# Softmax per 4 MB chunk read from PSUM, longer rows, fewer slots and a re-ordered head and tail in a one-core decode-attention kernel

## The chip, the cores and the metric

The kernel runs on one core of one Trainium2 chip. The metric is the device time of the whole program in microseconds, the median of several runs. The profile gives a span from the first to the last instruction, which is about 1.8 us shorter than the time (672.71 against 670.9 us for the kernel before).

Names used below. PE is the engine for matrix products, DVE the vector engine, ACT the scalar engine, SP the engine that issues the loads. "K31" and "V31" are the last 4 MB chunks of the two caches. A "landing" is the moment at which a load's completion count is full. A "tile" is 128 keys by 128 values. "P.V" is the product of the softmax weights P with V. The "early heads" are query heads 0 to 27, the "late heads" 28 to 31.

## The reference, cut to what matters

One token attends to a cache of 65,536 keys with 8 cache heads and 4 query heads for each. K and V together are 268 MB in bf16, and each byte is used once. The weights add 12 MB.

```
xn = layernorm(x)                                   # 512 values
q  = xn @ wq                                        # 32 heads of 128
scores = einsum(q, K) / sqrt(128);  p = softmax(scores)
o  = einsum(p, V)
out = x + o @ wo + (gelu(xn @ w1 + b1) @ w2 + b2)   # 512 values
```

## The kernel before

A small recording layer gives every operation its semaphore waits; the PE program of the steady state is folded into a hardware loop. For each tile of K, PE transposes it into PSUM, DVE or ACT copies it to SBUF, and PE multiplies it with the four queries. P.V uses each V tile as the weights. All loads are issued by SP, in order, as slots come free.

Before, K and V come in chunks of 2 MB (16 KB per partition), four of each make a unit, and softmax statistics are formed per unit of 256 tiles:

```python
BPC = 2; TPD = BPC * TPB; NC = 4                     # 64 tiles per chunk, 4 chunks per unit
slot = [kv[:, i*TPD*DH:(i+1)*TPD*DH] ... for i in range(2 * NC)]      # 8 slots of 2 MB

def scores(u, blk):
    ... pe.matmul(pss[sb][:, col*HPG:(col+1)*HPG], lhsT=kt_ring[...], rhs=q_cur) ...
    if blk % BPS == BPS - 1:
        dve.tensor_copy(out=scf[k][:, ...], in_=pss[sb])              # PSUM -> SBUF
        dve.tensor_reduce(out=pmax_parts[...], in_=dst, op=max)
...
# after the last unit (tail), in PE's order:
stats_1(); stats_2(L)
pv(0, 0); pv(0, 1)                                   # P.V of the last unit, chunk by chunk
... weights of all heads on DVE ...
pv(1, 0); pv(1, 1)
pv(2, 0)
wo_part(oT_bf, "oT", list(range(H)))                 # 128 matmuls
pv(2, 1); pv(3, 0); pv(3, 1)
... oL, wo_part of the last four heads, transpose, copy, store ...
```

## Time and profile before

| | before |
|---|---|
| time, median of 3 runs | 672.94 us (672.90 to 673.02) |
| span of the profiled run | 670.9 us |
| bytes read from HBM | 280.5 MB |
| PE busy | 83% |
| first load packet / last landing | 2.0 us / 665.2 us |
| tail after the last landing | 5.7 us |

The first lines are from the profile page of the kernel before: the busy time of each engine, and the rate of the loads in 40 equal slices of the span.

```profile
span 670.9 us, 27090 instructions
...
PE 556.9 (83%) x12746; PEld 540.2 (81%) x12746; DVE 288.2 (43%) x512; ACT 243.9 (36%) x325; POOL 1.3 (0%) x10
...
GB/s 375 414 424 422 427 422 425 429 427 429 420 420 429 425 429 413 426 431 427 426 415 425 430 425 428 415 426 430 427 426 430 428 427 426 428 427 428 427 429 206
```

The rate is flat: the loads are the bound, and only the first and the last slice are short. The stretches view says the same with finer windows. (In windows of a few microseconds it counts a packet whole, so that shares of 1.04 and 440 GB/s can appear, as from 5 to 10 us.) Its columns are the window in us, its length, the busy us and number of instructions of each engine, then the granted clock of PE, the busy share of the load engines, and GB/s.

```profile
core 0: us, PE busy (x) PEld busy (x) DVE busy (x) ACT busy (x) POOL busy (x), PEclk, DMA share, GB/s
100.00:200.00 100.00, 95.09 (x2091) 92.28 (x2089) 49.80 (x86) 43.54 (x59) 0.00 (x0) 0.77 1.01 425
...
500.00:600.00 100.00, 85.62 (x1953) 83.37 (x1952) 44.62 (x76) 40.33 (x56) 0.00 (x0) 0.78 1.01 427
...
655.00:660.00 5.00, 3.27 (x106) 3.18 (x103) 1.57 (x8) 0.00 (x0) 0.00 (x0) 0.50 1.00 423
660.00:665.00 5.00, 4.66 (x174) 4.67 (x175) 0.16 (x1) 0.00 (x0) 0.00 (x0) 0.50 0.47 193
```

The share is about 1 until 660 us. PE was not saturated: the waits view has it waiting for K chunks (columns: who waited for whom, us in total, times, longest).

```profile
PE pst L484 <- DMA kv<-in_A_k_cache_dram: 54.6, 22, 4.8
```

The last lines come from the timeline of PE and its neighbours at the end of the kernel before (columns: start, length, engine, line, operation; in brackets the idle time just before and what ended it).

```profile
660.34 1.02 PE L573 MATMUL pO<-P_bf,kv 128*128 128x4 bf16 x32 [2.07 <-DMA kv<-in_A_v_cache_dram]
...
664.63 2.70 PE L573 MATMUL pO<-P_bf,kv 128*128 128x4 bf16 x96
...
667.36 0.16 DVE L784 TENSOR_TENSOR oL_bf<-pO,coef 128x4 bf16<-128x4 f32 x1 [2.40 <-PE pO L573]
...
669.35 0.35 SPq L794 DMA_DIRECT2D out_dram<-fin_bf  x1
```

The wait for a V chunk ends at 660.34. The last 64 of the 96 matmuls at 664.63 are those of the chunk that landed at 665.2; they end at 667.3. The rest, to 670.9, is the last projection, the copy and the store.

The records of single load packets in the trace give the cost of a packet. This table is worked out from them; it is not a view of the profile.

```
kernel before: packet size, count, duration in ns
     4 B (completion count)    2164   median 9
  1024 B (wo)                  4096   min 46, median 48
 14336 B (w1, w2)               256   min 535, median 539
 16384 B (K, V)               16384   611 before compute starts; median 614, mean 616.7 over all
 32768 B (wq)                   128   1213 each
```

These fit 9 ns plus 27.2 GB/s for each of 16 load engines: an estimate from the table, since 2 x 611 - 1213 = 9 and 16,384 B in the other 602 ns are 27.2 GB/s.

### The profile page before, as it was taken

What the parts mean: (1) busy time and instruction counts of PE and PEld (TensorE: products, weight loads), DVE (VectorE), ACT (ScalarE), POOL (GpSimd) and SP (SyncE); (2) the same over time, 40 slices, a digit from 0 to 9 for tenths busy, and PEclk for the clock granted to TensorE, in tenths of its full rate; (3) what the DMA queues carried; (4) which work ended last, traced back from release to release, by engine and by line L of the source; (5) the groups of instructions that cost most, each with busy time, mean ns of one, the idle gap of its engine ahead of it and who ended that gap; (6) DMA issues with size and microseconds to landing.
All of it is one profiled execution on the core that took longest, in us unless ns stands there. A gap on an engine that the chain in (4) does not pass through costs nothing.

```text
span 670.9 us, 27090 instructions
## 1 busy us (share of the span) xinstructions
PE 556.9 (83%) x12746; PEld 540.2 (81%) x12746; DVE 288.2 (43%) x512; ACT 243.9 (36%) x325; POOL 1.3 (0%) x10
## 2 busy tenths in 40 slices
PE   0899979999998979779797788978889897898777
PEld 0898878989897878779787788877879787798766
DVE  0445434545554435345353444434444353454431
ACT  0233515353532425234261523515334161533330
POOL 0000000000000000000000000000000000000000
PEclk9876767979776778767687886678867797767965
DMA  8999999999999999999999999999999999999994
GB/s 375 414 424 422 427 422 425 429 427 429 420 420 429 425 429 413 426 431 427 426 415 425 430 425 428 415 426 430 427 426 430 428 427 426 428 427 428 427 429 206
DMA packets 23347, 280.82 MB, mean 419 GB/s; under 512 B 2458, under 2 KB 6556, under 8 KB 6556
## 3 DMA queue, kind: packets, MB, share of 16 engines
q1 hardware_dynamic: 23032, 280.50, 98.9%
q8 instruction: 15, 0.25, 0.1%
q10 hardware_dynamic: 292, 0.01, 0.0%
q14 instruction: 8, 0.07, 0.0%
HBM read 280.50 MB, written 0.00 MB: 418 GB/s over the span
## 4 chain that ended last, share of the span: by engine, by line
DMA 54%; PE 39%; ACT 6%; issue 1%; ACTq 0%; DVE 0%; SPq 0%
DMA kv<-in_A_k_cache_dram 49%; PE pst L484 26%; PE pO L573 5%; PE pss L505 5%; ACT P_bf L557 4%; DMA rows_bf<-in_B_b_dram 2%; ACT kt_ring L494 2%; DMA kv<-in_A_v_cache_dram 2%; PE pA L538 1%; PE pA L770 1%; PE pA L606 1%; PE pA L591 0%; PE pA L633 0%; ACTq L445 0%; PE pA L788 0%
## 5 line engine op out<-in xcount | busy, mean ns | idle before, releaser
L484 PE MATMUL pst<-ident_bf,kv 128*128 128x128 bf16 x4096 | 332.9, 255 | 80.1 <-DMA kv<-in_A_k_cache_dram 54.6
L484 PEld LDWEIGHTS pst<-ident_bf,kv 128*128 128x128 bf16 x4096 | 306.7, 117 | 90.6 <-issue 32.4
L494 ACT ACTIVATE kt_ring<-pst 128x1024 bf16<-128x1024 bf16 x192 | 194.7, 1022 | 381.7 <-PE pst L484 381.7
L492 DVE COPY kt_ring<-pst 128x1024 bf16<-128x1024 bf16 x320 | 213.1, 688 | 266.0 <-PE pst L484 265.6
L573 PE MATMUL pO<-P_bf,kv 128*128 128x4 bf16 x4096 | 117.1, 165 | 10.4 <-DMA kv<-in_A_v_cache_dram 4.9
L505 PE MATMUL pss<-q_cur,kt_ring 128*128 128x4 bf16 x4096 | 122.9, 165 | 1.4 <-issue 1.4
L573 PEld LDWEIGHTS pO<-P_bf,kv 128*128 128x128 bf16 x4096 | 111.8, 99 | 10.9 <-DMA kv<-in_A_v_cache_dram 5.2
L505 PEld LDWEIGHTS pss<-q_cur,kt_ring 128*128 128x128 bf16 x4096 | 118.7, 98 | 1.5 <-issue 1.5
L557 ACT ACTIVATE P_bf<-scf,negm 128x256 bf16<-128x256 f32 x64 | 49.6, 862 | 7.2 <-DVE negm L551 7.2
L513 DVE COPY scf<-pss 128x512 f32<-128x512 f32 x32 | 22.1, 692 | 64.5 <-PE pss L505 64.5
L517 DVE TENSOR_REDUCE pmax_parts<-scf 128x4 f32<-128x512 f32 x32 | 34.2, 1070 | 1.1
L457 PE MATMUL pA<-st,ones_f 128*128 128x2 f32 x2 | 0.6, 349 | 18.6 <-DVE st L455 18.6
L457 PEld LDWEIGHTS pA<-st,ones_f 128*128 128x128 f32 x2 | 0.5, 310 | 18.6 <-issue 18.6
L557 ACT ACTIVATION_READ_ACCUMULATOR P_bf<-scf,negm 128x1 f32 x64 | 13.6, 213 | 0.0
L538 PE MATMUL pA<-ident_f,pmax 128*4 128x128 f32 x32 | 8.5, 364 | 0.4 <-DVE pmax L525 0.4
L450 DVE CAST xT_f<-xT_bf 128x4 f32<-128x4 bf16 x1 | 0.2, 170 | 17.9 <-DMA rows_bf<-in_B_b_dram 17.9
L548 PEld LDWEIGHTS pA<-diag,ones_f 4*128 4x128 f32 x32 | 4.9, 190 | 2.7 <-DVE diag L542 1.1
L548 PE MATMUL pA<-diag,ones_f 4*128 4x4 f32 x32 | 6.3, 264 | 0.6 <-DVE diag L542 0.6
L468 ACT ACTIVATE mom<-mom 128x1 f32<-128x1 f32 x1 | 0.2, 203 | 16.3 <-DVE mom L466 16.3
L540 DVE TENSOR_REDUCE gmax<-pA 4x1 f32<-4x128 f32 x16 | 4.3, 269 | 0.6 <-PE pA L538 0.6
L582 DVE COPY o_all<-pO 128x4 f32<-128x4 f32 x15 | 2.3, 153 | 4.5 <-PE pO L573 4.5
L538 PEld LDWEIGHTS pA<-ident_f,pmax 128*4 128x4 f32 x32 | 1.4, 84 | 3.2 <-DVE kt_ring L492 2.5
(63 smaller groups left out, 50.1 us busy)
## 6 DMA issues: line engine op xcount, KB each, us to landing
kv<-in_A_k_cache_dram SPq DMA_DIRECT2D x64, 2048.0 KB, 31.6
kv<-in_A_v_cache_dram SPq DMA_DIRECT2D x64, 2048.0 KB, 33.8
kv<-in_A_wq_dram SPq DMA_DIRECT2D x1, 4096.0 KB, 17.1
wo_sb<-in_A_wo_dram SPq DMA_DIRECT2D x4, 1024.0 KB, 36.7
kv<-in_B_w_dram SPq DMA_DIRECT2D x2, 1792.0 KB, 27.7
xT_bf<-in_A_x_dram ACTq DMA_DIRECT2D x1, 1.0 KB
b1T_bf<-in_B_b_dram ACTq DMA_DIRECT2D x1, 3.5 KB
rows_bf<-in_A_x_dram ACTq DMA_DIRECT2D x1, 1.0 KB
```

What stands on the lines that cost most here:

```text
L484: lambda tb=tb, at=at, b=b, tt=s * TPB + t: pe.transpose(pst[tb][:, at * 128:(at + 1) * 128], slot[b][:, tt, :], ident_bf[:, :]),
L492: e, fn = DVE, lambda tb=tb, dst=dst: dve.tensor_copy(out=dst, in_=pst[tb][:, :])
L494: e, fn = ACT, lambda tb=tb, dst=dst: act.activation(out=dst, in_=pst[tb][:, :], func=ACTF.Copy)
L505: lambda sb=sb, col=col, kb=kb, t=t: pe.matmul(pss[sb][:, col * HPG:(col + 1) * HPG], lhsT=kt_ring[:, kb * BCOL + t * 128:kb * BCOL + (t + ...
L513: sch.op(DVE, lambda sb=sb, dst=dst: dve.tensor_copy(out=dst, in_=pss[sb][:, :]), reads=[f"pss{sb}"], writes=[f"scf{k}_{sb}"])
L517: lambda sb=sb, dst=dst: dve.tensor_reduce(out=pmax_parts[:, sb * HPG:(sb + 1) * HPG], in_=dst.rearrange("p (t j) -> p j t", j=HPG), axis= ...
L538: sch.op(PE, lambda: pe.matmul(pA[0:HPG, PA_ST:PA_ST + 128], lhsT=pmax[:, 0:HPG], rhs=ident_f[:, :], start=True, stop=True), reads=["pmax" ...
L548: sch.op(PE, lambda: pe.matmul(pA[:, PA_SB:PA_SB + HPG], lhsT=ones_f[0:HPG, 0:128], rhs=diag4[0:HPG, 0:HPG], start=True, stop=True), reads ...
L557: lambda k=k, u=u, j=j: act.activation(out=P_v[:, :, j], in_=scf_v[k][:, :, j], func=ACTF.Exp, bias=negm[:, u * HPG + j:u * HPG + j + 1], ...
L573: lambda b=b, tt=tt, gt=gt: pe.matmul(pO[:, 0:HPG], lhsT=slot[b][:, tt, :], rhs=P_v[:, gt, :], start=gt == 0, stop=gt == TPU - 1),
L606: lambda fc=fc, kt=kt: pe.matmul(pA[:, PA_H + fc:PA_H + fc + 1], lhsT=w1_sb[:, kt, fc:F:FC], rhs=xnT_bf[:, kt:kt + 1], start=kt == 0, stop ...
L770: lambda kt=kt, k=k, h=h: pe.matmul(pA[:, PA_AT + kt:PA_AT + kt + 1], lhsT=wo_sb[:, h, kt * 128:(kt + 1) * 128], rhs=rhs[:, k:k + 1], star ...
```

## The change

Its intent: fewer and longer load packets; no copy of the scores (the maximum and the exponentials read PSUM directly); PE starts on the first K chunk without waiting for layer norm; the last two V chunks use whatever slots are free; and the very last chunk arrives in pieces of 64, 32, 16, 8 and 8 tiles, so that little work is left after the last byte. The diff, cut to its core:

```diff
-    BPC = 2
+    BPC = 4                      # 128 tiles = 4 MB per chunk, 32 KB rows
-    NSLOT = 2 * NC               # 8 slots of 2 MB
+    NSLOT = 4                    # 4 slots of 4 MB
+    LASTP = (64, 32, 16, 8, 8)
+            if (kind, u) == ("V", NU - 1):      # last V chunk in falling pieces
+                for i, n in enumerate(LASTP):
+                    sch.dma(SP, ... slot[b][:, t0:t0 + n, :] ..., lsem[i], ...)
...
-            dve.tensor_copy(out=dst, in_=pss[sb][:, :])
-            dve.tensor_reduce(out=pmax_parts[...], in_=dst ...)
+            dve.tensor_reduce(out=pmax[:, :], in_=pss[k][:, 0:CW] ...)
-                    out=P_v[:, :, j], in_=scf_v[k][:, :, j], func=ACTF.Exp, ...   # 64 of 256 columns
+                    out=P_v[k][:, :, j], in_=src[:, :, j], func=ACTF.Exp, ...     # 128 of 128, from PSUM
...
+    # pair(i): two K chunks, two V chunks; the first pair transposes K before layernorm()
...
+    weights_1(*early)            # tail: "early" = heads 0 to 27, "late" = heads 28 to 31
+    stats_1()
+    weights_2(*early)
+    stats_2(L)
+    weights_3(*early)
+    merged(*early)
+    wo_part(*early)              # 112 matmuls
+    weights_1(*late)
+    pv(L - 1, range(TPD))        # P.V of V30
+    keep_o(L - 1)
+    ...
+    for i in range(len(LASTP)):  # P.V of V31, piece by piece
+        pv(L, range(cuts[i], cuts[i + 1]), f"last{i}")
+        if i == 0: wo_part(*late)
+        ...
```

## The prediction

> **What bounds the kernel now.** The DMA stream. In the stretches view the DMA share is 1.00 to 1.02 from 5 us to 660 us at 423 to 428 GB/s; 280.5 MB at that rate are 656 us of a 671 us span. The page's slices agree: only the first (375 GB/s) and last (206) are short. PE is 83% busy, but in the waits view it waited 54.6 us for K chunks, so it has slack. The queue never ran dry: a chunk's issue to landing was 7.8 us at least, 32 at the median. [...] So time per packet, the start and the tail count.
>
> **Time per packet.** In the trace's DMA packet records a 16 KB row took 611 ns before compute began and 616.7 ns on average later; the 32 KB rows of wq took 1213 ns each (all 128). 2 x 611 - 1213 = 9 ns, the time of one packet as such; a 4-byte semaphore packet also took 9 ns, and 1 KB took 46. So time = 9 ns + bytes at 27.2 GB/s per engine fits all sizes.
>
> **What the change does.**
> 1. 4 MB chunks with 32 KB rows: 16384 packets become 8192 on 16 engines: 8192 x 9 ns / 16 = 4.6 us less, and 64 fewer semaphore packets per engine, 0.6 us. If the 5.7 ns that compute adds to a packet is per packet rather than per byte, 2.9 us more. The last chunk's small pieces give 0.3 us back. Estimate: -6 us (-4.5 to -8).
> 2. Tail. The last piece landed at 665.2 us; 64 P.V matmuls ended at 667.3, the span at 670.9: 5.7 us. After: 8 P.V matmuls (estimate 0.4 us), oL 0.25, 16 matmuls of 128 columns at the half clock granted from 645 us on (1 to 1.9), one copy 0.35, out DMA 1.6. Estimate 4.4 us: -1.3 us.
> 3. Softmax from PSUM: 22 us of copies leave DVE, and exp becomes 128 x 256-to-128 column pieces, which adds some 20 us to ACT. Off the chain: 0.
> 4. K transposes first: PE starts at about 12 instead of 18.6 us. DMA is already queued for 38 us (16.2 MB), so 0 gained and nothing lost.
> 5. Four 4 MB slots: K(u+2) must be issued within about 29 us of K(u)'s landing; transposes take 8 (full clock) to 14 us (half clock). Some 13 us of slack remain: 0.
> 6. Start: first packet stays near 2.0 us: 0 to -0.5.
>
> **Predicted:** 672.9 - 6 - 1.3 = 665.6 us, range 662.5 to 669. Faster by over 2% (below 659.5) 6%, within 2% 92%, slower by over 2% 2%.
>
> **What would show it right.** 32 KB packets at 1216 to 1226 ns; steady rate 429 to 431 GB/s in the middle stretches; last landing near 659 to 660 us; 4 to 4.8 us after it; PE still waits for K chunks.
>
> **What would make it wrong.** If 32 KB rows under compute took 1233 ns (2 x 616.7), only the tail would be left: 671. If they ran at 1213 throughout, and the tail fell to 3 us, 659. If coarse slots let the queue run dry (DMA share below 0.97 in a middle stretch), slower. The 16 engines finish the last chunk between 661.2 and 665.2 us: if this skew shrinks or grows, the end moves by up to 2 us.

Remarks on it. "1.00 to 1.02 at 423 to 428 GB/s" holds for the stretches between 20 and 650 us; the short windows near the start show 0.98 to 1.04 and 420 to 440. With the bytes of each packet record spread over its duration, these windows give 428 to 432 GB/s. Last, its two clocks: in the trace of the kernel before, the clock records read 0.50 from 645.0 us to the end, and a transpose started every 55.9 ns at a granted clock of 1.00 and every 106.6 ns at 0.50, which is 7.2 and 13.6 us for the 128 of a chunk.

## The result and the profile after

| | before | after |
|---|---|---|
| time, median | 672.97 us (4 runs) | 671.02 us (670.45 to 671.21, 4 runs) |
| ratio | | 0.997 (0.9952 to 0.9987) |
| span of the profiled run | 670.9 us | 669.4 us |
| last landing | 665.2 us | 660.0 us |
| tail after it | 5.7 us | 9.4 us |

A ratio is the mean time of one kernel's fast runs over that of the other's in the same rounds, so it is not quite the ratio of the medians. The kernel is 0.3% faster; 665.6 us had been forecast.

The same lines of the page and of the stretches view, for the changed kernel:

```profile
span 669.4 us, 27324 instructions
...
PE 555.8 (83%) x12818; PEld 525.2 (78%) x12818; DVE 264.1 (39%) x548; ACT 243.5 (36%) x455; POOL 1.3 (0%) x10
...
GB/s 376 420 436 423 434 425 430 431 431 433 417 429 435 429 433 414 433 429 435 431 415 435 429 431 431 417 429 433 429 433 435 427 433 433 431 429 435 426 423 106
```

```profile
100.00:200.00 100.00, 91.49 (x2016) 86.20 (x2014) 43.79 (x86) 40.06 (x73) 0.00 (x0) 0.77 1.01 429
...
500.00:600.00 100.00, 86.41 (x1971) 81.69 (x1971) 41.08 (x82) 38.89 (x76) 0.00 (x0) 0.76 1.00 431
...
655.00:660.00 5.00, 2.95 (x111) 2.89 (x109) 0.63 (x6) 0.21 (x1) 0.00 (x0) 0.50 0.45 173
660.00:665.00 5.00, 4.95 (x162) 4.56 (x159) 1.77 (x13) 0.00 (x0) 0.00 (x0) 0.50 0.02 7
```

The five stretches from 100 to 600 us moved 425 to 427 GB/s before and 428 to 431 after, against a forecast of 429 to 431. The loads end early: in the stretch 660 to 665 the share is 0.02, where it was 0.47. In that same stretch PE is busy for 4.95 of 5 us. The packet records say why the stream is shorter: 32 KB packets took 1216 ns at the median and 1220.7 on average, and the durations of all K and V packets, the small pieces included, sum to 625.4 us per engine, against 631.5 before. The last landing came 5.2 us sooner. (The records overlap a little, as the share just above 1 shows, so their sum is not the time of the stream.)

PE still waits for K chunks, 88.8 us in all, of which 13.1 are for the very first chunk:

```profile
PE pst L477 <- DMA kv<-in_A_k_cache_dram: 88.8, 25, 13.1
```

The gain was lost behind the last landing. The granted clock of PE was 0.50 in both tails, so it does not make the difference. The timeline of PE in the tail of the changed kernel, with the two vector operations it turns on:

```profile
647.13 0.59 PE L518 MATMUL pA<-ident_f,pmax 128*4 128x128 f32 x2
...
648.41 0.77 PE L729 MATMUL pA<-sums,ones_f 128*128 128x112 f32 x2 [0.70 <-DVE gmax L520]
...
649.11 0.58 PE L528 MATMUL pA<-diag,ones_f 4*128 4x4 f32 x2
...
652.06 0.18 DVE L754 CAST oT_bf<-o_sum 128x28 bf16<-128x28 f32 x1
...
652.30 3.15 PE L763 MATMUL pA<-oT_bf,wo_sb 128*128 128x1 bf16 x112 [2.60 <-DVE oT_bf L754]
...
655.31 2.27 PE L552 MATMUL pO<-P_bf,kv 128*128 128x4 bf16 x80
...
659.63 1.42 PE L552 MATMUL pO<-P_bf,kv 128*128 128x4 bf16 x48 [2.05 <-issue]
...
660.91 0.59 PE L729 MATMUL pA<-sums,ones_f 128*128 128x16 f32 x2
...
661.34 1.85 PE L552 MATMUL pO<-P_bf,kv 128*128 128x4 bf16 x64
...
663.69 0.99 PE L552 MATMUL pO<-P_bf,kv 128*128 128x4 bf16 x32
...
665.15 1.01 PE L552 MATMUL pO<-P_bf,kv 128*128 128x4 bf16 x32
666.20 0.16 DVE L799 TENSOR_TENSOR oL_bf<-pO,coef 128x4 bf16<-128x4 f32 x1 [2.17 <-PE pO L552]
...
666.41 0.60 PE L803 MATMUL pss<-wo_sb,oL_bf 128*1 128x128 bf16 x16 [0.25 <-DVE oL_bf L799]
...
667.38 0.61 SPq L813 DMA_DIRECT2D out_dram<-fin_bf  x1
```

V30 landed at 650.03 us. PE did not touch it until 655.31: it stood idle from 649.70 to 652.30, because the next operation in its order was the output projection of the 28 early heads (L763, 112 matmuls), and that waited for DVE's merged vector, finished at 652.24. Then came its 3.15 us. After 80 of V30's 128 matmuls PE stood again for 2.05 us with the cause "issue". When the last piece landed at 660.02, PE still had part of V30 and all of V31 before it. It reached the end of V31 at 666.16, 6.1 us late.

### The profile page after: what moved, and what is told of

Read it like the earlier page. It is cut to its first block, busy times and chain, and to the rows that moved or that the text cites. A ratio compares the mean times of both kernels' runs of the same rounds, so it can differ in the third digit from the quotient of the medians.

```text
span 669.4 us, 27324 instructions
## 1 busy us (share of the span) xinstructions
PE 555.8 (83%) x12818; PEld 525.2 (78%) x12818; DVE 264.1 (39%) x548; ACT 243.5 (36%) x455; POOL 1.3 (0%) x10
## 4 chain that ended last, share of the span: by engine, by line
DMA 56%; PE 39%; issue 2%; ACT 1%; DVE 1%
DMA kv<-in_A_k_cache_dram 56%; PE pst L477 27%; PE pss L497 5%; PE pO L552 3%; PE pA L518 1%; PE pA L528 1%; PE pA L763 1%; PE pA L570 1%; PE pA L585 1%; ACT kt_ring L487 0%; PE pA L612 0%; ACT P_bf L538 0%; ACT L538 0%; ACT L462 0%; PE pA L729 0%
## 5 line engine op out<-in xcount | busy, mean ns | idle before, releaser
L477 PE MATMUL pst<-ident_bf,kv 128*128 128x128 bf16 x4096 | 314.5, 246 | 90.4 <-DMA kv<-in_A_k_cache_dram 88.8
L477 PEld LDWEIGHTS pst<-ident_bf,kv 128*128 128x128 bf16 x4096 | 286.3, 112 | 109.7 <-DMA kv<-in_A_k_cache_dram 77.7
L552 PE MATMUL pO<-P_bf,kv 128*128 128x4 bf16 x4096 | 120.4, 165 | 11.7 <-issue 11.7
L552 PEld LDWEIGHTS pO<-P_bf,kv 128*128 128x128 bf16 x4096 | 113.8, 100 | 12.6 <-issue 12.6
L505 DVE TENSOR_REDUCE pmax<-pss 128x4 f32<-128x512 f32 x32 | 22.1, 692 | 117.9 <-PE pss L497 117.9
L538 ACT ACTIVATE P_bf<-pss,negm 128x128 bf16<-128x128 f32 x128 | 50.8, 551 | 1.4 <-DVE negm L531 1.4
L538 ACT ACTIVATION_READ_ACCUMULATOR P_bf<-pss,negm 128x1 f32 x128 | 36.1, 282 | 0.0
L518 PE MATMUL pA<-ident_f,pmax 128*4 128x128 f32 x64 | 17.0, 363 | 0.0
L528 PE MATMUL pA<-diag,ones_f 4*128 4x4 f32 x64 | 12.4, 261 | 0.0
L528 PEld LDWEIGHTS pA<-diag,ones_f 4*128 4x128 f32 x64 | 9.6, 186 | 3.4 <-issue 0.2
L522 DVE TENSOR_SCALAR diag<-ident_f,gmax 4x4 f32<-4x4 f32 x32 | 7.0, 217 | 1.1
L763 PE MATMUL pA<-oT_bf,wo_sb 128*128 128x1 bf16 x128 | 3.7, 165 | 2.7 <-DVE oT_bf L754 2.6
L763 PEld LDWEIGHTS pA<-oT_bf,wo_sb 128*128 128x128 bf16 x128 | 3.6, 104 | 2.8 <-DVE oT_bf L754 2.7
L531 DVE TENSOR_SCALAR negm<-pA 128x4 f32<-128x4 f32 x32 | 5.1, 160 | 1.1 <-PE pA L528 1.1
```

The source lines that it names most:

```text
L477: lambda tb=tb, at=at, b=b, tt=s * TPB + t: pe.transpose(pst[tb][:, at * 128:(at + 1) * 128], slot[b][:, tt, :], ident_bf[:, :]),
L505: lambda k=k: dve.tensor_reduce(out=pmax[:, :], in_=pss[k][:, 0:CW].rearrange("p (t j) -> p j t", j=HPG), axis=AX.X, op=ALU.max),
L518: sch.op(PE, lambda: pe.matmul(pA[0:HPG, PA_ST:PA_ST + 128], lhsT=pmax[:, 0:HPG], rhs=ident_f[:, :], start=True, stop=True), reads=["pmax" ...
L528: sch.op(PE, lambda: pe.matmul(pA[:, PA_SB:PA_SB + HPG], lhsT=ones_f[0:HPG, 0:128], rhs=diag4[0:HPG, 0:HPG], start=True, stop=True), reads ...
L538: lambda k=k, u=u, j=j, src=src: act.activation(out=P_v[k][:, :, j], in_=src[:, :, j], func=ACTF.Exp, bias=negm[:, u * HPG + j:u * HPG + j ...
L552: lambda k=k, b=b, t=t: pe.matmul(pO[:, 0:HPG], lhsT=slot[b][:, t, :], rhs=P_v[k][:, t, :], start=t == 0, stop=t == TPD - 1),
```

## The experiments

Every experiment below is one edit to the changed kernel. "L763", "L552" and so on shift by a few lines where the edit adds lines. Diffs are cut to their core; lines that only move the loop or preset buffers are left out.

### 1. P.V of V30 ahead of the early heads

```diff
     merged(*early)
-    wo_part(*early)
     weights_1(*late)
     pv(L - 1, range(TPD))
     keep_o(L - 1)
+    wo_part(*early)
```

> One change to the changed kernel: in the tail, the P.V matmuls of the last chunk but one (V30, landed at 650.0 us in its trace) stand in PE's order before the 112 output-projection matmuls of the first 28 heads instead of after them. Theory A (the tail is PE working in order: it stood idle until 652.3 us for the merged vector of the early heads while V30 had landed): PE starts P.V at about 650.1 us, 2.2 us earlier, and as PE works without a gap to the end, the span falls from 669.4 to about 667.2 us (time about 668.8). The DMA's last landing stays at 660.0. Rival B (the end follows the landing of the last small pieces and their semaphores): no change, 671.0. Rival C (softmax from PSUM delays P of the last chunk, ready at 651.2 us): no change either, as that chunk's P.V come last anyway.

Measured: 669.30 us (669.01 to 669.61, 5 runs), ratio 0.9946 (0.9932 to 0.9959), span 667.7. The timeline of PE:

```profile
650.45 3.58 PE L552 MATMUL pO<-P_bf,kv 128*128 128x4 bf16 x128
...
653.89 1.84 PE L763 MATMUL pA<-oT_bf,wo_sb 128*128 128x1 bf16 x64
...
657.53 1.42 PE L763 MATMUL pA<-oT_bf,wo_sb 128*128 128x1 bf16 x48 [1.80 <-issue]
...
663.46 1.01 PE L552 MATMUL pO<-P_bf,kv 128*128 128x4 bf16 x32
```

V30's matmuls start at 650.45 and PE ends 1.7 us sooner, with the last landing unmoved at 660.06. The forecast of 668.8 was 0.5 us too good: the loop ended 0.8 us later in this run. The "issue" stall stayed at the same place in the code, not at the same operation: it came after 80 matmuls of V30 before, that is 112 + 80 = 192 matmuls after the three small ones, and now after 128 + 64 = 192. Rival B (the end follows the small pieces) and rival C (softmax from PSUM is late) foresaw no change. So the order alone was worth 1.7 us here.

### 2. The early heads left out of the tail (wrong result)

```diff
     merged(*early)
-    wo_part(*early)
     weights_1(*late)
```

> Wrong result on purpose: the 112 output-projection matmuls of the first 28 heads are left out of the tail (3.15 us on PE, after 2.6 us of waiting). Theory A: PE gains 5.2 us of order, so it catches up with the stream: span near 660.0 (last landing) + 0.4 + 3.2 (oL to the end, as in the trace of the changed kernel) = 663.7 to 664.5 us, time 665.3 to 666. The stall for PE instructions (2.05 us in the changed kernel) moves 112 matmuls later in the code and may lie in a wait for a piece. Rival B: the end stays about 9 us after the last landing, time 670 to 671.

Measured: 665.24 us (665.17 to 665.37, 4 runs), ratio 0.9887, span 663.4. (The comparison with the reference still passed: the part left out is smaller than its tolerance. So a passed comparison says nothing about the early heads in the other runs either.)

```profile
649.78 3.57 PE L552 MATMUL pO<-P_bf,kv 128*128 128x4 bf16 x128 [0.41 <-DMA kv<-in_A_v_cache_dram]
...
654.79 2.08 PE L552 MATMUL pO<-P_bf,kv 128*128 128x4 bf16 x64 [0.99 <-DVE coef L741]
...
659.77 0.38 PE L552 MATMUL pO<-P_bf,kv 128*128 128x4 bf16 x8 [0.27 <-DMA kv<-in_A_v_cache_dram]
...
660.40 0.59 PE L802 MATMUL pss<-wo_sb,oL_bf 128*1 128x128 bf16 x16 [0.25 <-DVE oL_bf L798]
```

Now PE waits for the loads again: 0.41 us for V30 and 0.27 us for the last piece, which landed at 659.72. (The 0.99 us at 654.79, for DVE's coefficients, did no harm: PE caught up.) The span ends 3.7 us after the landing. This is the tail that the prediction had costed, at 4.4 us. That the time comes so near the predicted 665.6 is in part luck: the landing was 0.5 us later than forecast (659.2) and the tail 0.7 us shorter. What the run shows is that the tail is 3.7 instead of 9.4 us once PE is rid of this work. It takes away three things at once: the wait for the early heads' vector, their 112 matmuls, and nearly all of the "issue" stall, since the instruction packet now comes at 654.31, while PE waits for the coefficients (0.16 us of stall is left). No run isolates the stall.

### 3. The last chunk in two pieces

```diff
-    LASTP = (64, 32, 16, 8, 8)
+    LASTP = (64, 64)
```

> One change to the changed kernel: the last V chunk comes in two pieces of 64 tiles instead of 64, 32, 16, 8, 8. Theory A: PE reaches the second half at 663.7 us in the changed kernel's trace, 3.7 us after everything has landed, so the falling pieces buy nothing there: time 671.0 within 0.4 us (less by up to 0.3 for fewer packets if anything). Rival B (the small pieces are what costs, by their packets and semaphores): faster by 1 us or more. The intent of the change (pieces shorten the tail): slower by about 1.5 us (56 more matmuls at 27 ns after the last landing).

Measured: 670.39 us (670.23 to 670.71, 5 runs), ratio 0.9963; the changed kernel had 0.997 in other rounds. The falling pieces buy nothing in the changed kernel. The time is 0.6 us less, 0.2 more than the limit that had been set, though the intervals of the two ratios overlap. The edit moves one thing more: the eight small matmuls of L795 stand after the second piece. That was in the middle of V31 (664.61 in the changed kernel, 0.61 us long); now it is behind V31, where PE waits for DVE in any case.

```profile
663.71 1.85 PE L552 MATMUL pO<-P_bf,kv 128*128 128x4 bf16 x64
...
665.49 0.61 PE L795 MATMUL pss<-ident_f,finT 128*1 128x128 f32 x8
```

V31 is finished at 665.56 here and at 666.16 in the changed kernel; the moved matmuls are enough to explain that, so a cost of the small pieces is not shown. This fits theory A and not the intent, under which two pieces should have cost 1.5 us.

### 4. 16 KB rows again

Each 4 MB chunk is loaded by two transfers, each of half the row.

```diff
-                sch.dma(SP, ... sp.dma_start(out=slot[b], in_=src), csem[b], ...)
+                hsem_n[b] += 32
+                for hf in range(2):
+                    ts = slice(hf * TPD // 2, (hf + 1) * TPD // 2)
+                    sch.dma(SP, ... sp.dma_start(out=slot[b][:, ts, :], in_=src[:, ts, :]),
+                            csem[b], ..., total=hsem_n[b])
```

> One change to the changed kernel: each 4 MB chunk is loaded by two transfers of half the row, so that the rows on the wire are 16 KB again (32 KB apart in memory). The packet model of the prediction (9 ns for each packet as such): 8064 more packets on 16 engines, plus 63 semaphore packets per engine, about 5.1 us more stream: last landing at 665.1 instead of 660.0 us, the tail behind it as long as before, time about 676. If row length does not matter for the rate and the earlier landing came from somewhere else (start, engine skew): last landing at 660 to 661, time 671 to 672.

Measured: 676.21 us (675.71 to 676.42, 4 runs), ratio 1.0047, last landing at 665.10 us, packets of 16 KB at 614 ns median and 617.1 mean. The stretches view has the old rates back (425 to 428 GB/s):

```profile
100.00:200.00 100.00, 86.13 (x1971) 81.28 (x1970) 41.73 (x82) 38.50 (x72) 0.00 (x0) 0.76 1.01 425
...
500.00:600.00 100.00, 85.89 (x1954) 80.98 (x1952) 40.81 (x80) 37.88 (x71) 0.00 (x0) 0.76 1.01 428
```

This is the packet term alone: 5.1 us more stream, as the model of 9 ns for each packet says (4.5 of it for rows, 0.6 for the completion packets of the doubled transfers, which this run does not separate), and a tail of 9.5 us as in the changed kernel. Fewer and longer packets are what shortened the stream; with the 16 KB rows back, the landing is that of the kernel before (665.2) in spite of the new slots, start and order.

### 5. A tail in the right order, first try

The weights, sums and merged vector of the early heads are computed inside each pair (only the last pair's result counts), and the 112 matmuls come right after the loop's statistics.

```diff
         scores(0, 1)
+        if not first:
+            weights_1(*early); weights_2(*early); weights_3(*early); merged(*early)
         v_block(ua - 2, 0)
...
-    weights_1(*early)
     stats_1()
-    weights_2(*early)
-    stats_2(L)
-    weights_3(*early)
-    merged(*early)
     wo_part(*early)
+    stats_2(L)
     weights_1(*late)
```

> The changed kernel with its tail put right: the weights of the 28 early heads, their sums and their merged vector are computed inside each pair (only the last pair's result is used), so that the 112 output-projection matmuls start as soon as the pair loop ends (about 647.5 us) and fill PE's wait for V30 (landed at 650.0 us). Theory A: PE reaches V30 at about 650.6 to 651 us, and, if the 2 us stall for PE instructions stands where it stood (192 matmuls behind the loop), catches up with the last piece about 1 us after its landing at 660.0: span 664 to 665, time 665.5 to 666.5. Rival (extra DVE and PE work in each pair pushes slots and so the stream back): last landing later than 660.5, DMA share under 1.00 in the middle stretches.

Measured: 668.75 us (668.47 to 669.18, 5 runs), ratio 0.994, span 666.7. This missed. Two things were seen. The 112 matmuls waited 0.37 us for the statistics, which use the same PSUM tile, `pA`:

```profile
649.78 3.14 PE L765 MATMUL pA<-oT_bf,wo_sb 128*128 128x1 bf16 x112 [0.37 <-DVE gmax L523]
```

And one load engine was 2.3 us later than the next at the end (completions of the last piece at 659.51 and then 661.84 us), and PE started on K31 1.8 us later than in the changed kernel; the loop ended 1.7 us later for it. Rates in the middle held, so the rival (extra work in each pair slows the stream) is not what the trace shows, but why this engine fell behind was not tested.

### 6. The same with 78 matmuls of no use at the start

The stall marked "issue" coincides with a 16 KB packet on the instruction queue q8 (at 657.14 us in the changed kernel; the next at 660.68 and 664.22). There is about one packet for every 128 matmuls: in the first 102 us of that kernel 12 packets came, the last after 1,560 matmuls, and the six stalls marked "issue" there stand 384, 247, 126, 249 and 126 matmuls apart. If such packets set the place of the stall, padding the PE program should move it.

```diff
+    for t in range(78):
+        pe.matmul(pO[:, 0:HPG], lhsT=ident_bf, rhs=ident_bf[:, 0:HPG], ...)
     marks = []
     pair(0)
```

> The same kernel with 78 matmuls of no use before the first transposes, where PE waits for the first chunk until 13 us. They only shift the PE program against the blocks in which its instructions are fetched (16 KB packets on the instruction queue, every 128 matmuls). If the stall's place is set by the block boundary, it moves by 78 matmuls: to 114 matmuls after the loop, or to 242 where PE waits for the first piece anyway (landed at 655.0 us). In the second case time 665.0 to 665.5, 0.3 to 1 us under the kernel without the padding; in the first the stall stays on PE's path and the time is that of the other, within 0.4 us. If the stall has nothing to do with block boundaries it stays at 192 matmuls.

Measured: 723.68 us (722.4 to 728.87, 5 fast runs), ratio 1.0777; a sixth run, 741.65, was slow (the median of all six is 724.72). Every forecast failed. The control below shows the same without the new tail.

### 7. The padding alone

The changed kernel with the 78 matmuls and nothing else.

> The changed kernel with the same 78 useless matmuls at the start and nothing else. Theory A: the tail's PE order is untouched, so the stall moves (from 80 P.V matmuls into V30 to 2 into V30, or into V31), but PE is late everywhere, so the time stays at 671.0 within 0.5 us, and the last landing at 660. If the early PE work at the start mattered (PE clock, order), the time would change by over 1 us.

Measured: 688.83 us (687.03 to 692.21, 3 fast runs), 2.4% above the kernel before; a fourth run, 698.83, is slow (the median of all four is 690.52, and the ratio, 1.0303, still counts that run). This failed too. From the load queues of its page (packets, MB, share of the load engines' time):

```profile
q8 instruction: 43, 0.70, 0.4%
```

And from the view of PE's waits:

```profile
PE pst L477 <- issue: 48.4, 14, 7.5
PE pO L552 <- issue: 19.1, 7, 3.7
...
PE pss L497 <- issue: 15.1, 9, 2.8
```

The instruction queue carried 43 packets; in the kernel before and the changed one it carried 15. The extra ones come while the loop runs, from 143 us on, and PE stood 82.6 us for "issue" in these three groups. Why the loop needs packets with the padding and none without is not in the trace.

### 8. Half the padding

Forty matmuls in place of 78.

> The changed kernel with 40 useless matmuls at the start in place of 78. With 78 the run had 43 instruction packets of 16 KB instead of 15 and took 690.5 us. Theory of the cliff [...]: with 40 [...] 15 instruction packets, time 671.0 within 0.5 us, and the stall after the loop moves from 192 to about 152 matmuls behind it. Rival (any useless matmul at the start does the harm, in proportion): about 680 us.

Measured: 672.17 us (670.93 to 673.22, 4 runs), ratio 0.9994 (0.9979 to 1.0009); span of the profiled run 668.9. The queue line of its page and two lines of PE's timeline:

```profile
q8 instruction: 15, 0.25, 0.2%
```

```profile
655.03 1.23 PE L552 MATMUL pO<-P_bf,kv 128*128 128x4 bf16 x41
...
658.01 2.48 PE L552 MATMUL pO<-P_bf,kv 128*128 128x4 bf16 x87 [1.75 <-issue]
```

Fifteen packets, as without padding, and the stall after 112 + 41 = 153 matmuls, where 152 had been forecast. So the stall moves with the padding (39 matmuls earlier for 40 put in ahead), and the harm is not in proportion to it: 40 cost about 1 us and no packet, 78 cost 17.8 us and 28 packets. The time missed its band: its runs spread over 2.3 us. Of this, 1.3 us lie in the spans (668.9 to 670.2) and the rest outside them (time less span is 2.0 to 3.0 us here, 1.8 in the other runs); nothing here explains either.

### 9. A tail in the right order, second try

The sums of the early heads are one more matmul in each pair; the vector work for them stands once, in the last pair, ahead of the last maximum, where DVE waits for scores (3.65 us before the last maximum in the changed kernel); the 112 matmuls come first after the loop.

```diff
         done_chunk("K", ub)
+        if not first:
+            weights_2(*early)
         scores(1, 1)
...
         v_block(ub - 2, 1)
+        if i == NU // 2 - 1:
+            weights_1(*early); weights_3(*early); merged(*early)
         scores(1, 3)
...
-    weights_1(*early)
+    wo_part(*early)
     stats_1()
-    weights_2(*early)
+    pv(L - 1, range(0, TPB))
     stats_2(L)
-    weights_3(*early); merged(*early); wo_part(*early)
     weights_1(*late)
-    pv(L - 1, range(TPD))
+    pv(L - 1, range(TPB, TPD))
```

> A second try at a tail that beats both kernels. The sums of the early heads are one more matmul in each pair, the vector work for the early heads stands once, in the last pair, where the vector engine waits for scores anyway; the 112 output-projection matmuls come first after the loop, before the statistics of the last chunk. Theory A: with K31 landing at about 630.6 us the loop ends at 647.1 to 647.5, the 112 matmuls run to 650.5, PE reaches V30 at once, and is through with the last piece 0.5 to 1.5 us after its landing at 660: span 664 to 665, time 665.6 to 666.6. If one DMA engine is late again, as in the first try (last landing 661.8 with the next engine at 659.5), the time is up to 667.5. Rival (the tail is bound by something else than PE's order): 668 or more.

Measured: 667.14 us (666.97 to 667.52, 5 runs), ratio 0.9916 (0.9903 to 0.993), correct by a comparison that does not see the early heads (experiment 2), last landing at 659.90.

```profile
647.67 3.12 PE L764 MATMUL pA<-oT_bf,wo_sb 128*128 128x1 bf16 x112
...
651.57 1.01 PE L553 MATMUL pO<-P_bf,kv 128*128 128x4 bf16 x32
...
654.84 1.42 PE L553 MATMUL pO<-P_bf,kv 128*128 128x4 bf16 x48 [0.37 <-issue]
...
661.01 1.01 PE L553 MATMUL pO<-P_bf,kv 128*128 128x4 bf16 x32
```

The 112 matmuls run where PE used to wait. This version beats both kernels: 3.9 us under the changed one and 5.8 under the one before. It is 0.5 us over its forecast band, since PE still finishes V31 at 662.0, 2.1 us after the landing: all of PE's work between 647.7 and 662.0 is needed, and only 1.2 us of that time were stalls or waits (0.26, 0.37 and 0.53).

## Why the prediction was wrong, point by point

- **What bounds the kernel: right.** The loads did, before and after, at a share of 1.00 to 1.01 in the middle.
- **Step 1, packets: right.** Forecast 6 us less (4.5 to 8), 429 to 431 GB/s and a last landing near 659 to 660 us; measured 5.2 us less, 428 to 431 GB/s and 660.0. Experiment 4 shows this term by itself. The extra time of a packet once compute runs: the mean rose from the 1213 ns of wq to 1220.7, 7.7 ns for 32 KB, where it was 5.7 for 16 KB (616.7 against 611), so here it goes neither purely with packets nor purely with bytes.
- **Step 2, tail: this is the step that failed.** The prediction wrote "8 P.V matmuls (estimate 0.4 us), oL 0.25, 16 matmuls", 4.4 us in all. It measured 9.4. The estimate counted only the work that needs the last piece and took for granted that PE had done all else by then. Experiment 2 gives PE that freedom and has a tail of 3.7 us. In the changed kernel, since V30's landing, PE had lost 2.3 us of waiting for the early heads' vector (2.6 in all), 3.15 us for their matmuls and 2.05 us marked "issue", so the tail was PE's queue of work and not the last piece. Experiment 1 takes 1.7 us back by order alone, experiment 9 takes 3.9. Of the small terms, the 16 matmuls were taken too high (1 to 1.9 us; measured 0.60), and the store too low (1.6 us; from its issue to the end of the span, about 2.0). In all, the span ended 5.8 us later than forecast: 0.8 from the stream and 5.0 from the tail.
- **Steps 3 to 6: right, as terms of no weight.** DVE's busy time fell from 288 to 264 us: the copies (22.1 us) went, and the maximum over the same 128x512 numbers took 692 ns from PSUM, where it had taken 1070 from SBUF. The exponentials and their sums took 86.9 us against 63.2 when their durations are added, but they overlap, and ACT's busy time stayed at 243.5. PE began at 13.1 us instead of 18.6 without gain, the slots kept the queue full.
- **What the prediction listed as dangers** (packet time, a dry queue, the skew of the engines) left out the one that came true. It had the means to see it: V30 lands one chunk (10 us) before the end, and the new PE order puts a chain of DVE operations and 112 matmuls in front of it.

The stall of 2 us: it comes with a packet on q8, about one for every 128 matmuls, each a weight load and a product (PE and PEld both count 12,818 instructions in the changed kernel). The packet behind the loop stopped PE for 2.05 us in the changed kernel, for 1.75 to 1.80 in experiments 1 and 8, and for 0.90 and 0.37 in experiments 5 and 9. In all of these PE's next matmul came 2.36 to 2.49 us after the start of the packet; what differs is how long before PE ran dry the packet started (0.44 us in the changed kernel, 1.46 and 2.02 in experiments 5 and 9). The packet after that one (at 660.68 in the changed kernel) stopped PE for nothing that the waits show. In the first 102 us of the changed kernel, six of the 12 packets came with a stall of PE, of 0.88 to 3.47 us, while the load share stayed at 1.00 (60 to 100 us). From 102 to 657 us, while its loop ran, q8 carried no packet. Why 40 matmuls ahead of the loop leave it so and 78 do not (15, 43 and, in experiment 6, 70 packets) was not shown.

The packet cost is 9 ns, a small part of the 611 ns of a 16 KB packet, and going from 16 to 32 KB still brought 5 us, 0.8% of the whole stream (last landing 665.1 us in experiment 4, 660.0 in the changed kernel).

Still open: why one load engine ends 2 to 4 us after the first. In the changed kernel the 16 completions of V31's last piece run from 655.8 to 660.0 us, ten of them over 1.5 us after the first; at 13 us those of K0 were within 0.55 us. Most of the spread is there by 93 us (3.64 us between the first and the last of the 16), in the time of the first 12 instruction packets, which suggests them, but no run tested it. Open too is why the padded loop had packets on q8 in some passes and none in others.

## What to carry to other kernels

Here, where a stream of loads was the bound, the end cost what the in-order engine still had queued at the last landing: the tail was 9.4 us with that queue and 3.7 without (experiment 2). So lay out that engine's order for the last two chunks against their landings before shortening the last piece. Work that needed only early data, put before the last loads into time that the engine waited anyway, took 3.9 us off (experiment 9): look for such time first. And 78 matmuls of no use ahead of a long PE loop, in idle time, took the packets on q8 from 15 to 43 and the time from 671.0 to 688.8 us, where 40 left the packets at 15 (experiments 7 and 8): count the packets on the instruction queue before and after any edit, even one that adds only idle-time instructions.
